# Attention followed by two FFN layers on one Trainium2 core: plain block products in the first set, and its first slot in the attention's tail

## The chip, the cores and the metric

One Trainium2 chip, of which the kernel uses 1 core. The metric is the device time of one execution in microseconds (us). The kernel before takes 961.27 us in the median of 3 runs (960.77 to 962.35).

## The reference

Forgetting attention over 4 batches, 8 heads, 576 tokens and 64 features per head, then two feed-forward layers without biases over the 2304 tokens of width 512, with 2048 hidden features each. All data are float32.

```python
# attention, per batch and head
scores = (q @ k.T) / 8 + cum[:, None] - cum[None, :]    # cum = cumsum(log(clip(f)))
attn = softmax(scores with the upper triangle masked)
x = attn @ v                                            # laid out as 2304 tokens x 512
# first layer
h = x @ w_in                                            # 2304 x 2048
x = (h - tanh(h)) @ w_out
# second layer
h = x @ w_in2
out = (h * sigmoid(h)) @ w_out2
```

## The kernel before

**Precision.** Every operand of a feed-forward product is split into a high part (rounded to the matmul's reduced float32) and a low part, the remainder. Each product is three matmuls: high by high, high by low, low by high. Making the split costs a copy with rounding on ScalarE (`xo` L270, `wh` L188, `gh` L393) and a subtraction on VectorE (`xo` L271, `wl` L190, `gl` L397).

**Attention.** `attention` (L465) walks over 16 pairs of heads, 9 score tiles to a pair, in one loop over steps `n` (L818). Scores on TensorE (L579, L587), row minima on VectorE (L600), exponentials on ScalarE (L608), scaling by the row sums on GpSimd (L622), transposes on TensorE (L634) whose results VectorE and ScalarE copy out (`ptf`, L679), products with the values on TensorE (L690), and a copy into `x` (L698). Steps past the last tile form its tail: the last pairs' transposes and values. The table `ahead` (L790) hangs other work on steps counted from the end of the tiles (`n - N`): loading and decoding the first weights, opening pools in the room that the attention gives up, making the first operands, and the first pieces of the first slot (`next, first`).

**Weights.** They arrive as 64-bit numbers and are decoded by `wjob` (L146): `scale` on ScalarE (L153), `shift`, `exponent`, `low` and `join` on VectorE (L157 to L172), then the splits `hi` and `lo`. For `w_in`, four sums of blocks come between (`sum`, L177). One *pair* of weights (index `q`) is 256 hidden features: `w_in` (m = 0) and `w_out` (m = 1). Two pairs make a *set*; a layer has four sets.

**Slots.** A *unit* is one set by one block of 768 tokens, so a set has three units, and layer 1 and layer 2 have twelve each. A *slot* is one unit by one pair; there are 48 slots, numbered from 0, so the first set is slots 0 to 5. In each slot the product of `w_in` with `x` is cut into 2 by 2 blocks and done in Winograd's form with **seven** block products (`product`, L366; six matmuls of 384 columns each) instead of eight: seven sums of operands made in advance (`xtemp`, `xmake`: `xt` L257, `xo` L270 and L271) and seven additions per slot on VectorE behind the products (`add`, L407) plus one copy on ScalarE (L435). `bend` (L381) applies tanh to a half of 768 elements (L384) and subtracts (L386). Eight steps of the second product (`project`, L322, six matmuls each) of the slot before stand between the block products, as the letters P and G in `slot_steps` (L409) say:

```python
pieces = "P1 G P6 G P2 G G P7 G P5 G P4 G P3 G".split()
if sl == 0:
    pieces = "P1 P2 P6 G G G G P7 G P5 G P4 G P3 G".split()
```

In slot 0 nothing is there to project, in slot 1 only two of the eight steps are. The seven operands of a block are made once, in the first set, spilled to DRAM (`xd`, L273), and reloaded for the later sets (`xload`, L278).

**What sets the order.** The program is scheduled by hand: every engine and every DMA queue runs its instructions in the order in which the code emits them. `fills` hands out the decoding of later weights to positions in slots, `xplan` (filled by `xat`, L287 on) the making and reloading of operands. All bulk transfers stand in the queue of SyncE (SP).

## Time and profile before

| | |
|---|---|
| runs, median of 3 | 961.27 us (960.77 to 962.35) |
| the profiled execution, its own time | 961.22 us |
| its span in the profile | 959.4 us |
| mean granted TensorE clock | 0.995 |
| PE busy | 930.7 us (97%) |
| VectorE (DVE) busy | 741.3 us (77%) |
| ScalarE (ACT) busy | 438.1 us (46%) |
| GpSimd (POOL) busy | 161.2 us (17%) |
| DMA engines, mean busy share of the main queue | 53.7% |
| of the chain that ended last: PE, DVE, ACT | 84%, 9%, 3% |

The profiled execution's own time is 1.8 us more than its span. PE is TensorE's matmuls, PEld its weight loads; a matmul's end is modelled, so matmuls that follow one another overlap in the table, and the spacing of starts tells the rate. The attention takes the first 180 us or so, the first layer runs to about 570 us, and the second layer takes the rest.

### The profile page before, as it was taken

What the parts mean: (1) busy time and instruction counts of PE and PEld (TensorE: products, weight loads), DVE (VectorE), ACT (ScalarE), POOL (GpSimd) and SP (SyncE); (2) the same over time, 40 slices, a digit from 0 to 9 for tenths busy, and PEclk for the clock granted to TensorE, in tenths of its full rate; (3) what the DMA queues carried; (4) which work ended last, traced back from release to release, by engine and by line L of the source; (5) the groups of instructions that cost most, each with busy time, mean ns of one, the idle gap of its engine ahead of it and who ended that gap; (6) DMA issues with size and microseconds to landing.
All of it is one profiled execution on the core that took longest, in us unless ns stands there. A gap on an engine that the chain in (4) does not pass through costs nothing.

```text
span 959.4 us, 14837 instructions
## 1 busy us (share of the span) xinstructions
PE 930.7 (97%) x5496; PEld 844.5 (88%) x5496; DVE 741.3 (77%) x1338; ACT 438.1 (46%) x782; POOL 161.2 (17%) x242
## 2 busy tenths in 40 slices
PE   8999999769999999999999989999999999999998
PEld 6777776559999999999999989898998999898996
DVE  7788887888897887888788988877767677764543
ACT  6788879445554332424233435564423243332311
POOL 8999998200000000000000000000000000000000
PEclk9999999998999999999999999999999999999999
DMA  5344353544576565756585354657756485437622
GB/s 172 135 131 133 112 174 125 208 176 173 235 283 242 180 237 208 275 184 234 174 314 196 136 210 153 230 218 275 306 187 213 164 315 209 161 135 230 236 94 98
DMA packets 45800, 188.86 MB, mean 197 GB/s; under 512 B 9440, under 2 KB 9440, under 8 KB 45696
## 3 DMA queue, kind: packets, MB, share of 16 engines
q1 hardware_dynamic: 45720, 187.90, 53.7%
q8 instruction: 43, 0.70, 0.3%
q14 instruction: 29, 0.24, 0.1%
q10 hardware_dynamic: 8, 0.02, 0.0%
HBM read 148.44 MB, written 38.34 MB: 195 GB/s over the span
## 4 chain that ended last, share of the span: by engine, by line
PE 84%; DVE 9%; ACT 3%; issue 2%; POOL 1%; DMA 1%; ACTq 0%; POOLq 0%; DVEq 0%
PE a L342 37%; PE h L374 32%; PE t L634 4%; PE s L587 4%; PE out_t L690 4%; DVE hs L407 2%; PE s L579 2%; DVE xo L271 1%; ACT t L384 1%; DVE wl L190 1%; DVE xt L257 1%; ACT xo L270 1%; DVE t L386 1%; POOL p L622 1%; ACT wh L188 1%
## 5 line engine op out<-in xcount | busy, mean ns | idle before, releaser
L374 PE MATMUL h<-xo,wh 128*128 128x384 f32 x1344 | 346.2, 338 | 12.1 <-DVE hs L407 6.9
L374 PEld LDWEIGHTS h<-xo,wh 128*128 128x128 f32 x1344 | 246.7, 189 | 29.6 <-DVE hs L407 7.2
L407 DVE TENSOR_TENSOR hs<-h,hs 128x384 f32<-128x384 f32 x336 | 186.0, 554 | 87.1 <-PE h L374 82.0
L384 ACT ACTIVATE t<-hs 128x768 f32<-128x768 f32 x96 | 81.3, 847 | 339.7 <-DVE hs L407 339.4
L374 PE MATMUL h<-xo,wl 128*128 128x384 f32 x672 | 226.6, 337 | 0.0
L342 PE MATMUL a<-gh,wl 128*128 128x384 f32 x384 | 129.2, 337 | 2.6 <-DVE wl L190 2.6
L342 PE MATMUL a<-gl,wh 128*128 128x384 f32 x384 | 129.0, 336 | 1.9 <-DVE gl L397 1.9
L342 PE MATMUL a<-gh,wh 128*128 128x384 f32 x384 | 129.2, 336 | 0.3 <-DVE x L358 0.3
L374 PEld LDWEIGHTS h<-xo,wl 128*128 128x128 f32 x672 | 126.9, 189 | 0.0
L397 DVE TENSOR_TENSOR gl<-t,gh 128x768 fp32r<-128x768 f32 x96 | 91.6, 954 | 37.6 <-ACT gh L393 37.4
L342 PE MATMUL a<-wh,gl 128*128 128x512 f32 x288 | 114.1, 396 | 0.0
L342 PE MATMUL a<-wl,gh 128*128 128x512 f32 x288 | 113.8, 395 | 0.0
L342 PE MATMUL a<-wh,gh 128*128 128x512 f32 x288 | 112.1, 389 | 0.6 <-DVE ob L362 0.6
L393 ACT CAST gh<-t 128x768 fp32r<-128x768 f32 x96 | 80.3, 837 | 29.6 <-DVE t L386 28.5
L608 ACT ACTIVATE p<-p,mn 128x128 f32<-128x128 f32 (+3 forms) x128 | 71.3, 559 | 14.7 <-DVE mn L600 12.6
L342 PEld LDWEIGHTS a<-gh,wl 128*128 128x128 f32 x384 | 72.6, 189 | 2.9 <-DVE wl L190 2.9
L600 DVE CUSTOM_DVE_ANT_0 p<-s,mask 128x128 f32<-128x128 f32 (+3 forms) x128 | 59.5, 480 | 19.9 <-PE s L587 19.9
L342 PEld LDWEIGHTS a<-gl,wh 128*128 128x128 f32 x384 | 72.5, 189 | 2.1 <-DVE gl L397 2.1
L622 POOL TENSOR_SCALAR p<-p,sm 128x128 f32<-128x128 f32 (+3 forms) x128 | 72.1, 581 | 11.6 <-DVE sm L619 11.5
L342 PEld LDWEIGHTS a<-gh,wh 128*128 128x128 f32 x384 | 72.6, 189 | 1.0 <-DVE x L358 0.9
L386 DVE TENSOR_TENSOR t<-hs,t 128x768 f32<-128x768 f32 x48 | 46.0, 958 | 25.5 <-ACT t L384 23.3
L342 PEld LDWEIGHTS a<-wh,gl 128*128 128x128 f32 x288 | 54.0, 187 | 11.6
(90 smaller groups left out, 1230.9 us busy)
## 6 DMA issues: line engine op xcount, KB each, us to landing
xo<-xd SPq DMA_DIRECT2D x126, 768.0 KB
xd<-xo SPq DMA_DIRECT2D x42, 768.0 KB
raw<-w_in SPq DMA_DIRECT2D x32, 512.0 KB
raw<-w_out SPq DMA_DIRECT2D x32, 512.0 KB
kqraw<-kq SPq DMA_DIRECT2D x16, 608.0 KB
vraw<-v SPq DMA_DIRECT2D x16, 320.0 KB
out<-ob SPq DMA_DIRECT2D x6, 512.0 KB
out<-ob SPq DMA_DIRECT2D x6, 256.0 KB
```

The costliest lines, as they stand in the source:

```text
L342: nc.tensor.matmul(dst, w, m, start=first and r == 0, stop=last and r == 2)
L374: nc.tensor.matmul(dst, w[:, ks], m[:, k], start=k == 0 and r == 0, stop=k == 1 and r == 2)
L384: nc.scalar.activation(t, hs[h], AF.Silu if l else AF.Tanh)
L386: nc.vector.tensor_tensor(t, hs[h], t, ALU.subtract)
L393: nc.scalar.copy(gh, hs[h])
L397: nc.vector.tensor_tensor(gl, hs[h], rd(gh), ALU.subtract)
L407: nc.vector.tensor_tensor(to, p, s, ALU.add)
L587: nc.tensor.matmul(s[:, h, c:c + n], a[half(h), q], b[half(h), 0:n], start=r == 0, stop=r == 3,)
L600: nc.vector.tensor_tensor_reduce(out=pt.rearrange("p (g c) -> p g c", g=2) if i == 4 else pt, in0=src, in1=m, op0=ALU.add, op1=ALU.min, sc ...
L608: nc.scalar.activation(pt, pt, AF.Exp, bias=mn, scale=-1.0, accum_out=sums[:, n // 3 % 5, n % 3, 0:1],)
L622: nc.gpsimd.tensor_scalar(pt, pt, sm[:, j:j + 1], 1.0, ALU.mult, ALU.mult)
L634: nc.tensor.transpose(t[:, k], pt[:, c * P:c * P + P], ident)
```

## The change

It does five things, all around the first set.

1. In slots 0 to 5 the 2 by 2 blocks are multiplied plainly: **eight** block products (`plain`), accumulated two by two in PSUM, with no sums of weights, no sums of operands and no additions behind them. tanh and the subtraction now work on quarters of 384 elements straight from PSUM. The order of pieces in these slots is one product, one G, eight times.
2. All of slot 0 is emitted inside the attention's tail (16 pieces instead of 3), and with it three operands that are blocks of `x` (operand 0 is new, held in the tile of operand 7).
3. The decoding of the second pair moves: its `w_in` into the attention's steps (in halves of 512 elements), its `w_out` into the tail. The loads of the first four weights are asked for earlier, and the block sums of the first two pairs are gone.
4. The seven Winograd operands are still made and spilled, for the later sets, but spread over slots 0 to 4 (`STAGED`, `STAGED_AT`), partly in other operands' tiles: operand 5 of the first unit in tile 6, operand 7 always in tile 5.
5. The reloads of the fourth unit (in slot 5) are asked for in the order 6, 4, 1, 5, 2, 7, 3. Pools open at other steps, and some are split.

```diff
         e, o, k = 2 * s + 2, 2 * s + 3, 6 * s
...
+        if s == 0:
+            plan = {
+                1: jobs(e, 0, SCALING, PRE[:2]),
+                2: jobs(e, 0, PRE[2:], SUMS),
+                3: jobs(e, 0, HILO) + jobs(e, 1, SCALING, PRE[:1]),
+                4: jobs(e, 1, PRE[1:], LAST),
+                5: jobs(o, 0, SCALING, PRE, SUMS, HILO) + jobs(o, 1, SCALING),
+                6: jobs(o, 1, PRE),
+            }
...
-    fills[0] = jobs(1, 1, [("scale",)], PRE)
-    fills[1] = jobs(1, 1, LAST)
...
+    STAGED = ((xtemp, 1), (xmake, 5), (xtemp, 2), (xmake, 6), (xtemp, 4), (xmake, 4), (xtemp, 3), (xmake, 7, None, 5))
+    STAGED_AT = (
+        (None, None, None, None, (1, 1), (1, 3), (1, 6), (1, 9)),
+        ((2, 3), (2, 5), (2, 9), (2, 11), (2, 13), (2, 15), (3, 1), (3, 3)),
+        ((3, 10), (3, 12), (4, 1), (4, 3), (4, 5), (4, 7), (4, 9), (4, 11)),
+    )
...
     for u, (l, s, b) in enumerate(units):
-        if u == 0:
+        if u < NB:
+            if u:
+                for p, i, *place in ((5, 1), (7, 2), (13, 0, None, 7), (15, 3)):
+                    xat(2 * u - 1, p, xmake, u, i, *place)
+            for k, to in enumerate(STAGED_AT[u]):
+                if to:
+                    xat(*to, *staged(u, k))
+            continue
+        if u == NB:
+            for i, p in ((6, 0), (4, 1), (1, 4), (5, 5), (2, 6), (7, 12), (3, 14)):
+                xat(2 * u - 1, p, xload, u, i)
             continue
...
+    def plain(u, j, r, h, k):
+        q = 2 * (u // NB) + j
+        c = ((1, 2), (3, 0))[r][k]
+        wih, wil = (w[:, c] for w in wtiles[q, 0])
+        xh, xl = (xo[u, ((1, 7), (2, 3))[k][h]][:, e] for e in range(2))
+        if k == 0:
+            hs[h, r] = pools["ps_h"].tile([P, 512], F32, tag="h", name=f"h{u}_{j}_{h}_{r}")[:, 0:TH]
+        dst = hs[h, r]
+        for d in range(2):
+            ds = slice(d * P, d * P + P)
+            for n, (w, m) in enumerate(((wih, xh), (wih, xl), (wil, xh))):
+                nc.tensor.matmul(dst, w[:, ds], m[:, d], start=k == d == n == 0, stop=k == d == 1 and n == 2)
+        if k == 0:
+            return
+        if r == 0:
+            hs[h] = pools["tp"].tile([P, 2, TH], F32, tag=f"t{h}", name=f"t{u}_{j}_{h}")
+        t = hs[h][:, 1 - r]
+        nc.scalar.activation(t, dst, AF.Tanh)
+        nc.vector.tensor_tensor(t, dst, t, ALU.subtract)
...
-        if sl == 0:
-            pieces = "P1 P2 P6 G G G G P7 G P5 G P4 G P3 G".split()
+        if u < NB:
+            pieces = [c for r in ("000", "001", "100", "101", "010", "011", "110", "111") for c in (r, "G")]
...
+            elif u < NB:
+                r, h, k = map(int, what)
+                plain(u, j, r, h, k)
+                if p == 0:
+                    rest()
+                elif p in (6, 14):
+                    left.extend([(high, (u, j, h)), (low, (u, j, h))])
+                    if p == 6:
+                        rest()
...
-            for n, q, m, i in ((27, 0, 0, 0), (31, 0, 0, 1), (54, 0, 1, 0), (58, 0, 1, 1), (112, 1, 0, 0),
-                               (114, 1, 0, 1), (121, 1, 1, 0), (123, 1, 1, 1)):
+            for n, q, m, i in ((22, 0, 0, 0), (24, 0, 0, 1), (54, 0, 1, 0), (58, 0, 1, 1), (85, 1, 0, 0),
+                               (87, 1, 0, 1), (112, 1, 1, 0), (114, 1, 1, 1)):
...
+            todo = jobs(0, 0, scales, both, PLAIN) + jobs(0, 1, scales, both)
+            todo += [(0, 1, w, i) for w in ("hi", "lo") for i in range(2)] + jobs(1, 0, scales, both)
             for k, job in enumerate(todo):
-                at(NTILE * (4 + k // 3) + (1, 3, 5)[k % 3] - N, wjob, *job)
+                at(NTILE * (3 + k // 3) + (1, 3, 5)[k % 3] - N, wjob, *job)
...
+            inner = {
+                2: jobs(1, 0, PLAIN[:1]), 3: jobs(1, 1, SCALING) + jobs(1, 0, PLAIN[1:2]),
+                4: jobs(1, 0, PLAIN[2:]) + jobs(1, 1, PRE[:1]), 5: jobs(1, 1, PRE[1:2]),
+                6: jobs(1, 1, PRE[2:3]), 7: jobs(1, 1, PRE[3:]),
+            }
...
+            for n, k in ((3, 2), (4, 4), (5, 2), (6, 3), (7, 2), (8, 3)):
+                for _ in range(k):
+                    at(n, next, first)
```

**TensorE in the tail, around the values of the last pair.** Names: `h` is a product's result, `t_3` the last pair's last transposes, `out_15` and `out_t` the last pair's products with the values (`ptf` by `vraw`). Before, three block products stand ahead of them and the fourth (`h_0_7`) follows:

```order
L634 MATMUL t_3_1_2920<-ident,pt_1_107 128x128
L374 MATMUL h_0_6_2935<-xo_6_2865,wh_0_1579 128x384 x2
L374 MATMUL h_0_6_2935<-xo_6_2865,wl_0_1580 128x384
L374 MATMUL h_0_6_2935<-xo_6_2865,wh_0_1579 128x384 x2
L374 MATMUL h_0_6_2935<-xo_6_2865,wl_0_1580 128x384
L690 MATMUL out_15_2943<-ptf_110,vraw_2689 64x64 x2
L690 MATMUL out_t<-ptf_110,vraw_2689 64x512 x2
L690 MATMUL out_t<-ptf_110,vraw_2689 64x448 x2
L690 MATMUL out_t<-ptf_110,vraw_2689 64x320 x2
L690 MATMUL out_t<-ptf_110,vraw_2689 64x192 x2
L690 MATMUL out_t<-ptf_110,vraw_2689 64x64 x2
L374 MATMUL h_0_7_3002<-xo_7_2959,wh_0_1579 128x384 x2
```

With the change (`h_0_1_0` is half 1, row 0 of slot 0; lines have moved):

```order
L423 MATMUL h_0_1_0_2974<-xo_7_2838,wl_0_1200 128x384
L423 MATMUL h_0_1_0_2974<-xo_3_2875,wh_0_1199 128x384 x2
L423 MATMUL h_0_1_0_2974<-xo_3_2875,wl_0_1200 128x384
L423 MATMUL h_0_1_0_2974<-xo_3_2875,wh_0_1199 128x384 x2
L423 MATMUL h_0_1_0_2974<-xo_3_2875,wl_0_1200 128x384
L747 MATMUL out_15_2990<-ptf_105,vraw_2694 64x64 x2
L747 MATMUL out_t<-ptf_105,vraw_2694 64x512 x2
L747 MATMUL out_t<-ptf_105,vraw_2694 64x448 x2
L747 MATMUL out_t<-ptf_105,vraw_2694 64x320 x2
L747 MATMUL out_t<-ptf_105,vraw_2694 64x192 x2
L747 MATMUL out_t<-ptf_105,vraw_2694 64x64 x2
L423 MATMUL h_0_1_1_3004<-xo_7_2838,wh_0_1199 128x384 x2
```

Six of slot 0's eight products stand ahead of the last values, and the other two behind them; before it was three of seven.

**VectorE at the end of slot 1, before.** Names: `hs` and `t` are the halves of h and of its tanh, `gl` the low part of the activation, `xo_*` the operands of the second unit, `wl_1_3100` the low part of the second pair's `w_out`:

```order
L386 TENSOR_TENSOR t_1_0_3133<-hs_1_0_3062,t_1_0_3133 128x768
L271 TENSOR_TENSOR xo_5_3136<-xt_1_1_3082,xo_5_3136 128x768
L257 TENSOR_TENSOR xt_1_1_3082<-x 128x768
L407 TENSOR_TENSOR hs_1_1_3080<-h_1_3_3149,hs_1_1_3080 128x384
L397 TENSOR_TENSOR gl_1_0_3158<-t_1_0_3133,gh_1_0_3157 128x768
L386 TENSOR_TENSOR t_1_1_3161<-hs_1_1_3080,t_1_1_3161 128x768
L271 TENSOR_TENSOR xo_7_3164<-xt_1_1_3082,xo_7_3164 128x768
L190 TENSOR_TENSOR wl_1_3100<-wa_1_3020,wh_1_3099 128x1024
L397 TENSOR_TENSOR gl_1_1_3187<-t_1_1_3161,gh_1_1_3186 128x768
L271 TENSOR_TENSOR xo_4_3190<-xt_1_2_3084,xo_4_3190 128x768
L407 TENSOR_TENSOR hs_0_1_3208<-h_0_6_3201,hs_0_0_3184 128x384
L271 TENSOR_TENSOR xo_3_3210<-x,xo_3_3210 128x768
```

With the change the low part of the second pair's `w_out` (`wl_1_3052`) is in slot 0, before slot 0's second `gl`, and the operands near it (`xt_0_2`, `xo_6`) are the first unit's, for the later sets:

```order
L452 TENSOR_TENSOR gl_0_0_2963<-t_0_0_2928,gh_0_0_2962 128x768
L736 COPY ptf_105<-t_3_1_2943 128x2x64
L164 SCALAR_TENSOR_TENSOR wb_1_2947<-raw_1_2247,wb_1_2947 128x1024
L267 TENSOR_TENSOR xt_0_2_2972<-x,xt_0_1_2897 128x768
L430 TENSOR_TENSOR t_0_1_2987<-h_0_1_0_2974,t_0_1_2987 128x384
L172 TENSOR_TENSOR wa_1_2920<-wa_1_2920,wb_1_2947 128x1024
L281 TENSOR_TENSOR xo_6_3013<-xt_0_2_2972,xo_6_3013 128x768
L430 TENSOR_TENSOR t_0_1_2987<-h_0_1_1_3004,t_0_1_2987 128x384
L193 TENSOR_TENSOR wl_1_3052<-wa_1_2920,wh_1_3051 128x1024
L452 TENSOR_TENSOR gl_0_1_3063<-t_0_1_2987,gh_0_1_3062 128x768
```

The split of that weight has moved from behind slot 1's products, fourth from the end, to the middle of slot 0.

**ScalarE in the tail.** `ptf` are the copies of transposed tiles that the values wait for. Before:

```order
L679 COPY ptf_110<-t_1_0_2870 128x2x2x128
L679 COPY ptf_110<-t_2_0_2894 128x2x2x128
L270 CAST xo_5_2924<-xt_0_1_2834 128x768
L679 COPY ptf_110<-t_3_0_2915 128x4x2x64
L698 COPY x<-out_15_2943 128x64
L698 COPY x<-out_t 128x512
L270 CAST xo_7_2959<-xt_0_1_2834 128x768
L188 CAST wh_0_2986<-ws_0_2882 128x768
L270 CAST xo_4_2989<-xt_0_2_2836 128x768
```

With the change (`t_0_0`, `t_0_1` written from `h` are tanh of slot 0, `gh` its rounding):

```order
L736 COPY ptf_105<-t_1_0_2883 128x2x2x128
L429 ACTIVATE t_0_0_2928<-h_0_0_0_2899 128x384
L736 COPY ptf_105<-t_2_0_2906 128x2x2x128
L280 CAST xo_6_2949<-xt_0_1_2897 128x768
L429 ACTIVATE t_0_0_2928<-h_0_0_1_2931 128x384
L448 CAST gh_0_0_2962<-t_0_0_2928 128x768
L736 COPY ptf_105<-t_3_0_2938 128x4x2x64
L429 ACTIVATE t_0_1_2987<-h_0_1_0_2974 128x384
L755 COPY x<-out_15_2990 128x64
L755 COPY x<-out_t 128x512
L280 CAST xo_6_3013<-xt_0_2_2972 128x768
L429 ACTIVATE t_0_1_2987<-h_0_1_1_3004 128x384
```

Between the copies of `t_1_0` and `t_3_0` there stood one operand's cast; now there are two tanh, a cast and a rounding.

## Rows read from the trace of the kernel before

**Rows 1.** The page: busy time of each engine over the span.

```profile
PE 930.7 (97%) x5496; PEld 844.5 (88%) x5496; DVE 741.3 (77%) x1338; ACT 438.1 (46%) x782; POOL 161.2 (17%) x242
```

**Rows 2.** Busy time by stretch: start:end, length, then busy (instructions) of each engine, clock, DMA.

```profile
138.65:148.54 9.89, 9.89 (x93) 7.46 (x90) 9.55 (x34) 8.37 (x26) 9.81 (x15) 1.00 0.56 170
148.54:158.42 9.88, 9.06 (x84) 6.84 (x80) 7.18 (x27) 9.19 (x26) 9.58 (x13) 1.00 0.30 105
172.30:206.00 33.70, 25.34 (x139) 21.17 (x139) 28.09 (x40) 16.08 (x23) 3.01 (x2) 0.95 0.47 183
206.00:231.00 25.00, 19.18 (x93) 18.38 (x93) 21.16 (x29) 10.73 (x14) 0.00 (x0) 0.86 0.47 190
231.00:246.60 15.60, 15.60 (x92) 15.60 (x91) 14.28 (x22) 10.01 (x14) 0.00 (x0) 1.00 0.58 220
```

**Rows 3.** Waits of PE, 170 to 232 us: total, times, longest.

```profile
PE h L374 <- DVE hs L407: 6.9, 5, 3.4
...
PE a L342 <- DVE wl L190: 2.6, 1, 2.6
...
PE a L342 <- DVE gl L397: 1.9, 1, 1.9
...
PE t L634 <- ACT ptf L679: 0.6, 1, 0.6
```

**Rows 4.** Timeline of PE: start, length, instruction, idle before it.

```profile
165.03 1.25 PE L634 MATMUL t<-ident,p 128*128 128x128 f32 x10
...
172.32 0.85 PE L634 MATMUL t<-ident,p 128*128 128x128 f32 x6 [1.44 <-ACT x L698]
...
178.69 2.76 PE L690 MATMUL out_t<-ptf,vraw 128*64 128x512 f32 x20
...
196.40 1.01 PE L374 MATMUL h<-xo,wh 128*128 128x384 f32 x2 [3.42 <-DVE hs L407]
...
215.10 0.44 PE L342 MATMUL a<-gl,wh 128*128 128x384 f32 x1 [1.88 <-DVE gl L397]
...
218.17 0.69 PE L342 MATMUL a<-gh,wl 128*128 128x384 f32 x1 [2.62 <-DVE wl L190]
```

**Rows 5.** Chain that ended last, third slot's end: start, length, what.

```profile
229.92 1.04 PE a L342 x6
230.96 1.04 PE h L374 x6
```

**Rows 6.** Waits of PE from 231 us to the end.

```profile
PE h L374 <- ACT xo L270: 2.0, 1, 2.0
```

**Rows 7.** Groups by line and shape, whole run: xcount | busy, mean ns | idle.

```profile
L407 DVE TENSOR_TENSOR hs<-h,hs 128x384 f32<-128x384 f32 x336 | 186.0, 554 | 87.1 <-PE h L374 82.0 <-ACT xo L270 1.0
...
L397 DVE TENSOR_TENSOR gl<-t,gh 128x768 fp32r<-128x768 f32 x96 | 91.6, 954 | 37.6 <-ACT gh L393 37.4
...
L384 ACT ACTIVATE t<-hs 128x768 f32<-128x768 f32 x96 | 81.3, 847 | 339.7 <-DVE hs L407 339.4 <-ACT gh L393 0.3
...
L386 DVE TENSOR_TENSOR t<-hs,t 128x768 f32<-128x768 f32 x48 | 46.0, 958 | 25.5 <-ACT t L384 23.3
...
L177 DVE TENSOR_TENSOR ws<-ws 128x256 f32<-128x256 f32 x64 | 26.7, 438 | 0.3
...
L271 DVE TENSOR_TENSOR xo<-xt,xo 128x768 fp32r<-128x768 f32 x24 | 22.9, 956 | 4.8 <-ACT xo L270 4.8
...
L435 ACT COPY hs<-h 128x384 f32<-128x384 f32 x48 | 22.5, 468 | 5.9 <-PE h L374 5.6
...
L164 DVE SCALAR_TENSOR_TENSOR wb<-raw,wb 128x1024 f32<-128x1024 uint32 x30 | 36.9, 1230 | 0.5
...
L190 DVE TENSOR_TENSOR wl<-wa,wh 128x1024 fp32r<-128x1024 f32 x15 | 18.3, 1219 | 1.3 <-ACT wh L188 1.3
...
L164 DVE SCALAR_TENSOR_TENSOR wb<-raw,wb 128x512 f32<-128x512 uint32 x4 | 3.5, 868 | 0.0
```

**Rows 8.** Chain that ended last, a spill to DRAM: start, length, what.

```profile
212.75 3.29 DMA xd<-xo
```

More of the change, by code (lines that the diff above doesn't have):

```diff
@@ L59, in forgetting_attention_two_ffn @@
     dram = ctx.enter_context(tc.tile_pool(name="dram", bufs=1, space=bass.MemoryType.DRAM))
-    wpool = {0: ctx.enter_context(tc.tile_pool(name="wp0", bufs=1))}
+    wpool = dict.fromkeys(((0, 0), (0, 1)), ctx.enter_context(tc.tile_pool(name="wp0", bufs=1)))
     def rd(ap):
@@ L181, in wjob @@
                 wtiles[q, m] = [
-                    wpool[q % NSLOT].tile(shape, F32R, tag=f"w{s}{q % NSLOT}_{m}", name=f"w{s}{n}") for s in "hl"
+                    wpool[q % NSLOT, m].tile(shape, F32R, tag=f"w{s}{q % NSLOT}_{m}", name=f"w{s}{n}") for s in "hl"
                 ]
@@ L185, in wjob @@
             frm = st["s"][:, 1:8] if m == 0 else st["w"]
-            c = i if m else (slice(0, 3), slice(3, 7), slice(3, 5), slice(5, 7))[part]
+            c = i if m else (slice(0, 3), slice(3, 7), slice(3, 4))[part]
+            if m == 0 and part == 2:
+                frm = st["s"][:, 0:1]
+            frm = frm if m == 0 and part == 2 else frm[:, c]
             if what == "hi":
-                nc.scalar.copy(hi[:, c], frm[:, c])
+                nc.scalar.copy(hi[:, c], frm)
             else:
-                nc.vector.tensor_tensor(lo[:, c], frm[:, c], rd(hi[:, c]), ALU.subtract)
+                nc.vector.tensor_tensor(lo[:, c], frm, rd(hi[:, c]), ALU.subtract)
     PRE = [(w,) for w in ("shift", "exponent", "low", "join")]
@@ L390, in high @@
         slot = gfree.pop(0)
-        gh, gl = (pools["gp"].tile([P, 2, TH], F32R, tag=f"g{s}{slot}", name=f"g{s}{u}_{j}_{h}") for s in "hl")
+        gh, gl = (pools[f"gp{slot // 2}"].tile([P, 2, TH], F32R, tag=f"g{s}{slot}", name=f"g{s}{u}_{j}_{h}") for s in "hl")
         gt[u, j, h] = gh, gl, slot
@@ L466, in attention @@
         with ExitStack() as actx:
-            early, earlier = (actx.enter_context(ExitStack()) for _ in range(2))
+            mid, early, earlier = (actx.enter_context(ExitStack()) for _ in range(3))
             def pool(stack, name, bufs=1, **kw):
@@ L486, in attention @@
             raw, vraw, kqs = {}, {}, {}
+            ptfs = [pl.tile([P, 2, NPT], F32, name=f"ptf{i}") for i, pl in ((1, ptps[1]), (0, ptps[0]))][::-1]
             des = [kp.tile([P, S + 512], F32R, name=f"de{i}") for i in range(2)]
@@ L494, in attention @@
             out_0 = {}
-            ptfs = [ptp.tile([P, 2, NPT], F32, name=f"ptf{i}") for i in range(2)]
             def half(h):
@@ L814, in attention @@
-            for job in jobs(1, 0, SUMS):
-                at(6, fill, job)
-            for n in (3, 4, 6):
-                at(n, next, first)
+                at(NTILE * (3 + k // 3) + (1, 3, 5)[k % 3] - N, wjob, *job)
+            for n, i, eng, place in ((-11, 1, nc.gpsimd, 1), (-8, 2, nc.gpsimd, 2), (1, 0, None, 7), (2, 3, None, 3)):
+                at(n, xmake, 0, i, eng, place)
+            at(-2, wload, 2, 0)
+            inner = {
[3 more added lines that the diff above has]
+            }
@@ L847, in forgetting_attention_two_ffn @@
         attention(slots[0])
-        for (q, m, *what), i in zip(jobs(1, 0, HILO), (4, None, 3, None)):
-            wjob(q, m, *what)
-            if i:
-                xmake(0, i)
+        for job in jobs(1, 1, LAST):
+            wjob(*job)
         for slot in slots:
```

86 lines of the change are left out of this document (43 added, 43 removed).

## Prediction

> **What bounds the kernel now.** I read the busy line of the page first: TensorE is busy 97% of the span and no other engine over 77% [rows 1]. So the question is where TensorE is not served, and whether the change serves it there. The busy time by stretch answers the first half [rows 2]. In the attention TensorE is full in a pair's 9.89 us (the pair at 138.65), and from 231 us on it is full again. Between 172.3 and 231.0 it is not: 25.3 of 33.7 us, then 19.2 of 25.0. VectorE is at 28.1 and 21.2 us there, the highest of the others. After 231 us TensorE's longest wait is one of 2.0 us, at the second layer's start [rows 6], which the change does not touch.
>
> The waits of TensorE between 170 and 232 us name VectorE: 6.9 us for the additions behind the products (`hs`), 2.6 us for the split of the second pair's `w_out` (`wl`), 1.9 us for the low part of an activation (`gl`) [rows 3]. The timeline shows the long ones at 196.40, 215.10 and 218.17 us [rows 4]. It also shows the clock: the mean granted clock is 0.95 and 0.86 in the two stretches and 1.00 after them [rows 2]. It fell to its lower level, 1.2 GHz, after TensorE had waited 3.42 us at 196.40, and again after the waits before 218.17.
>
> What TensorE's work in this place needs comes from its own rate. Six matmuls of 384 columns take 1.04 us at the full 2.4 GHz [rows 5], so one takes 0.1733 us. From 172.32 us, where the last pair's second transposes start [rows 4], to 230.96 us, where the third slot's last six matmuls have ended and the fourth slot starts [rows 5], the program has 19 transposes (10 took 1.25 us, so 2.4 us), the last pair's values (0.17 us and 2.76, 2.9 us) [rows 4], and 186 matmuls: 42 + 42 + 42 block products and 12 + 48 projections, 32.2 us. That is 37.5 us of work in 58.6 us. **21.1 us are lost to waiting and to the slow clock.**
>
> **The change, part by part.**
>
> *Eight products for seven.* Six slots get 6 matmuls more each: 36 by 0.1733 = 6.2 us more for TensorE. 18 of them (3.1 us) lie in slots 0 to 2, in the stretch that loses 21.1 us; the other 18 (3.1 us) lie in slots 3 to 5, where TensorE is full, and they cost what they take.
>
> *Additions gone.* Each of the six slots loses seven additions of 554 ns, and two subtractions of 958 ns become four on quarters, which I price by the addition that also reads PSUM, 554 ns [rows 7]: 3.9 + 1.9 - 2.2 = 3.6 us less on VectorE per slot, 21.5 us in all. ScalarE loses a copy of 468 ns and two tanh of 847 ns, and gets four of a quarter. A quarter's tanh is nowhere in the trace: the copy of the same 384 elements from PSUM took 468 ns, half of a whole tanh is 424. I take 468, so 1.9 us replace 2.2.
>
> A rule weighs in here against the change. The rows say that two quarters cost VectorE 1.1 us where the whole cost 0.96. The Trainium skill (Perfetto Trace Analysis, section Optimizing Scalar/DVE Operations) says that each ScalarE and VectorE instruction pays a fixed access cost and that larger operations pay where such an engine is saturated. By that rule alone, cutting the tanh work would lose about 0.3 us of VectorE per slot; by the rows the seven additions that go outweigh it twelve times, and the sum keeps the rows.
>
> *Operands and sums.* Eight block sums of weights of 438 ns go (3.5 us). Three splits of operand 0 come, 956 ns each on VectorE (2.9 us) [rows 7]. The seven Winograd operands per block are still made, but no product of the first set waits for them, so they may be late; their cover is the set itself, and if it is gone the fourth unit's reloads in slot 5 are late.
>
> *The second pair's decoding.* Its `w_in` goes into the attention's last four pairs in halves, at most three instructions a pair; a half's costliest step is 868 ns where a whole one took 1230 [rows 7]. Three such are 2.6 us. I cost them at nothing, because the pair at 138.65 already carries three decoding steps and keeps its 9.89 us, and in the one that follows VectorE is busy only 7.2 of 9.88 us [rows 2]. Without that cover it would be up to 2.6 us for each of two pairs. Its `w_out` goes into the tail: the split that TensorE waited 2.62 us for at 218.17 [rows 4] is emitted a slot and a half earlier and stops being a wait.
>
> *Slot 0 in the tail.* On TensorE 36 instead of 18 matmuls stand ahead of the last values (3.1 us more), so these end later. Only the room that they free waits for them, and the data of the first units are of batches done long before. On ScalarE two tanh and a rounding now stand in front of the copy `t_3_0` that the values need. Going through the queue from 172.3 us with the durations of [rows 7], the copy is done about when TensorE comes to the values, so that wait is a few tenths. The one like it before was 0.6 us [rows 3].
>
> *SP's queue.* It holds 64 weight loads, 42 spills and 126 reloads as before. A weight load that waits for its room has behind it only spills that VectorE makes later still.
>
> **The sum.** VectorE's 35 instructions from 172.7 us to slot 1's end: 8 quarters (4.4), 4 `gl` (3.8), 8 operand splits (7.6), 3 operand sums (2.9), copies of the tail (1.4), weight splits (2.5), decoding (5.2): 27.8 us. TensorE's work there is 2.4 + 2.9 + 108 by 0.1733 = 24.0 us. So VectorE is the longer one by 4 us, but its last ten instructions serve products half a slot or more later, and in slot 2 it has some 14 us against TensorE's 16.6 (96 matmuls). The one place with little room is the second unit's second operand, VectorE's 27th instruction: 21.5 us of work after 172.7 is 194.2 us, and TensorE wants it two products into slot 2, at 172.3 + 24.0 + 2.1 = 198.4. VectorE lost 5.6 us to waits in this stretch before (33.7 - 28.1 [rows 2]); as much again makes 199.8, 1.4 us late. With 0.6 us for the copy in the tail I keep **2.0 us** of waiting.
>
> TensorE then reaches the end of slot 2 at 172.3 + 37.5 + 3.1 + 2.0 = 214.9 us instead of 230.96. What followed took 959.4 - 230.96 = 728.4 us, and gets 3.1 us more: 946.5 us of span. With the 1.8 us that lie around it this execution would have taken **948.3 us** instead of 961.22; the median of the runs shown, 961.27, is the same within 0.05. With no wait at all it is 946.3. If the wait of 1.44 us at 172.32 for ScalarE [rows 4], where a different cast now stands in the way, went too, 944.9: the low end.
>
> **The rivals.**
>
> *A wait takes the old one's place.* ScalarE and VectorE alternate within each quarter (tanh, subtraction, rounding, low part), each in order, so one late operand holds up the next quarter. For it: VectorE is still the longer engine in slots 0 and 1. If TensorE waits as at 215.10 and 218.17 (1.9 + 2.6 us), and its clock falls as there, it also pays 2.7 us for the clock (the third slot's 25.0 us less 15.6 of work, less 1.5, 2.2 and 2.9 us of gaps). That is 7.2 us: 946.3 + 7.2 = 953.5. Against it: four PSUM buffers let TensorE run half a slot ahead.
>
> *Late reloads.* The first operand that slot 6 needs is now third in line instead of first, behind operands 6 and 4 and two weight loads. A transfer of this size took 3.29 us on the chain [rows 8]. One such late: 948.3 + 3.3 = 951.6. Against it: 11 us of slot 5 are left after its request.
>
> *Slower.* A staging tile is written again while its spill is under way: tile 6 once in slot 0, tile 5 four times in slots 1 to 4. The cast that rewrites it waits in ScalarE's queue with the tanh behind it. If each of the five waited a whole transfer and TensorE with it, that is 5 by 3.29 = 16.5 us: 948.3 + 16.5 = 964.8. It decides from 3 us a piece on, where it eats the gain. For it: the chain itself runs over such a spill [rows 8]. Against it: eight VectorE instructions, some 6 us, lie between the two writes of tile 6, and more between the others.
>
> *It only moves the loss.* TensorE gets its 6.2 us and VectorE's relief turns into waits for ScalarE of the size of the gain: 961.
>
> **How the numbers follow.** The forecast (945 to 950) has 0.68, because its gain is TensorE's own lost time, counted from two points of the timeline. The wait in the old one's place has 0.17, late reloads 0.07, slower 0.04, no difference 0.04. 0.2% (1.9 us) is about what a measurement of this kernel can tell from no change. Faster is 0.68 + 0.17 + 0.07 = 0.92, the same 0.04, slower 0.04. The range goes from 944.9, the sum without either wait, to 954.5, just over the first rival; it leaves out the last two cases and the edges.
>
> **What would show it.** Right: the stretch from 172 to 231 us has TensorE full from the first slot's end, with no granted clock under 1.00; no wait for `hs` or for the second pair's `wl`; TensorE's matmul count up by 36; the pairs of the attention still 9.89 us. Wrong: waits of TensorE over 2 us in slots 1 and 2, for `xo` or for PSUM freed by the quarter subtractions; a wait for a reload at slot 6's start; casts of operands 5 and 6 on ScalarE that wait for a DMA; a longer pair in the attention's last four.

## The result, and the profile after

The changed kernel took **948.51 us** (median of 4 runs, 948.34 to 949.93) where the kernel before, on the same chip, took 961.81 us (4 runs, 960.77 to 964.13): a ratio of 0.9864, 95% interval 0.9851 to 0.9877, 13.3 us less. Forecast were 948.3 us, faster. The profiled execution took 948.34 us with a span of 946.3 us.

The page's busy line and the busy time by stretch, in the columns of [rows 1] and [rows 2]. The first two stretches are the two pairs of the attention; the next three are what lies between the last pair's second transposes and slot 1, then slot 1, then slot 2.

```profile
PE 932.3 (99%) x5532; PEld 848.5 (90%) x5532; DVE 720.1 (76%) x1306; ACT 437.8 (46%) x791; POOL 159.4 (17%) x242
```

```profile
138.65:148.54 9.89, 9.89 (x93) 7.46 (x91) 8.84 (x33) 8.06 (x26) 9.21 (x15) 1.00 0.39 126
148.54:158.42 9.88, 9.06 (x83) 6.85 (x80) 8.82 (x30) 8.52 (x24) 9.88 (x13) 1.00 0.10 37
171.22:185.35 14.13, 13.95 (x91) 11.88 (x92) 12.00 (x17) 8.34 (x17) 2.01 (x2) 1.00 0.41 162
185.35:195.75 10.40, 10.40 (x61) 10.40 (x61) 7.32 (x10) 7.14 (x10) 0.00 (x0) 1.00 0.57 230
195.75:213.49 17.74, 16.93 (x98) 16.61 (x98) 16.40 (x24) 9.46 (x15) 0.00 (x0) 1.00 0.65 256
```

TensorE has 36 instructions more, VectorE 32 fewer. The pairs keep their 9.89 us. Slots 0 to 2, where the clock had been granted at 0.95 and 0.86 [rows 2], now run at 1.00, and slot 1 is full. TensorE's waits in this place, to be read against [rows 3]:

```profile
PE a L377 <- ACT x L391: 0.8, 1, 0.8
PE t L691 <- DVE ptf L736: 0.6, 1, 0.6
PE out_t L747 <- ACT ptf L736: 0.2, 1, 0.2
```

The waits for `hs`, `wl` and `gl` are gone, and so is one that [rows 3] does not show, of 1.57 us at 183.01 for ScalarE's cast of an operand:

```profile
183.01 0.44 PE L374 MATMUL h<-xo,wh 128*128 128x384 f32 x1 [1.57 <-ACT xo L270]
```

The timeline of TensorE places the three that are left, and two more at the second layer's start, which answer to [rows 6]:

```profile
171.22 1.04 PE L691 MATMUL t<-ident,p 128*128 128x128 f32 x6 [0.64 <-DVE ptf L736]
...
180.43 2.81 PE L747 MATMUL out_t<-ptf,vraw 128*64 128x512 f32 x20 [0.18 <-ACT ptf L736]
...
210.25 0.44 PE L377 MATMUL a<-gh,wh 128*128 128x384 f32 x1 [0.81 <-ACT x L391]
...
554.26 0.45 PE L409 MATMUL h<-xo,wh 128*128 128x384 f32 x1 [2.03 <-ACT xo L280]
555.25 0.69 PE L409 MATMUL h<-xo,wh 128*128 128x384 f32 x1 [0.55 <-DVE xo L281]
```

The tanh and the subtraction of a quarter, in the columns of [rows 7]:

```profile
L430 DVE TENSOR_TENSOR t<-h,t 128x384 f32<-128x384 f32 x24 | 13.3, 554 | 3.8 <-ACT t L429 3.7
L429 ACT ACTIVATE t<-h 128x384 f32<-128x384 f32 x24 | 11.8, 490 | 9.6 <-PE h L423 9.4
```

**Where the time went.** The last pair's second transposes start at 171.22 us, 1.1 us sooner than in [rows 4]. The chain that ended last puts the end of slot 2 at 213.65 us, where it stood at 230.96 [rows 5] (the timeline has both 0.16 us sooner, at 213.49 and 230.80):

```profile
213.65 1.04 PE h L423 x6
```

From 171.22 on that is 42.4 us for 40.7 us of work (the 37.5 us of before and 18 matmuls). So 1.8 us are lost where 21.1 were. After that the 18 matmuls of slots 3 to 5 cost 3.1 us. The same product that waits at the second layer's start came at 568.71 us before and comes at 554.26 now: 14.45 us sooner. From there to the end it is 390.7 us before and 392.0 now: 1.35 us are given back behind that wait, and 13.1 us of span are left.

The time from that product to the end is used below as a second measure: "layer change" is when it starts, in the one profiled execution of each kernel. It leaves out what happens behind it, which varies (last section). The medians include it: a run without the fall of the clock behind the layer change is shorter by a us or more, and the changed kernel's four runs all have a mean granted clock of 0.998 or less.

### The profile page after: what moved, and what is told of

The parts are those of the page before. It is cut to its first block, busy times and chain, and to the rows that moved or that the text cites. A ratio compares the mean times of both kernels' runs of the same rounds, so it can differ in the third digit from the quotient of the medians.

```text
span 946.3 us, 14874 instructions
## 1 busy us (share of the span) xinstructions
PE 932.3 (99%) x5532; PEld 848.5 (90%) x5532; DVE 720.1 (76%) x1306; ACT 437.8 (46%) x791; POOL 159.4 (17%) x242
## 4 chain that ended last, share of the span: by engine, by line
PE 85%; DVE 7%; POOL 3%; ACT 2%; issue 2%; DMA 1%; SPq 0%; DVEq 0%; ACTq 0%; POOLq 0%
PE a L377 38%; PE h L409 30%; PE t L691 4%; PE s L644 4%; PE out_t L747 4%; PE h L423 3%; PE s L636 2%; DVE xo L281 1%; POOL p L679 1%; DVE hs L462 1%; POOL kqs L586 1%; DMA xo<-xd 1%; DVE xt L267 1%; DVE gl L452 1%; ACT xo L280 1%
## 5 line engine op out<-in xcount | busy, mean ns | idle before, releaser
L409 PE MATMUL h<-xo,wh 128*128 128x384 f32 x1176 | 300.9, 336 | 3.1 <-ACT xo L280 2.0
L409 PEld LDWEIGHTS h<-xo,wh 128*128 128x128 f32 x1176 | 215.7, 188 | 18.2 <-ACT xo L280 2.6
L462 DVE TENSOR_TENSOR hs<-h,hs 128x384 f32<-128x384 f32 x294 | 163.0, 555 | 88.9 <-PE h L409 85.2
L439 ACT ACTIVATE t<-hs 128x768 f32<-128x768 f32 x84 | 71.2, 847 | 312.5 <-DVE hs L462 312.5
L409 PE MATMUL h<-xo,wl 128*128 128x384 f32 x588 | 197.9, 336 | 0.0
L409 PEld LDWEIGHTS h<-xo,wl 128*128 128x128 f32 x588 | 110.7, 188 | 0.0
L448 ACT CAST gh<-t 128x768 fp32r<-128x768 f32 x96 | 80.3, 837 | 35.7 <-DVE t L441 23.8
L665 ACT ACTIVATE p<-p,mn 128x128 f32<-128x128 f32 (+3 forms) x128 | 71.2, 558 | 15.6 <-DVE mn L657 12.6
L393 DVE TENSOR_TENSOR x<-a,x 128x768 f32<-128x768 f32 (+2 forms) x60 | 57.1, 951 | 9.4 <-PE a L377 9.3
```

What stands on the lines that cost most here:

```text
L393: nc.vector.tensor_tensor(total, acc, total, ALU.add)
L409: nc.tensor.matmul(dst, w[:, ks], m[:, k], start=k == 0 and r == 0, stop=k == 1 and r == 2)
L439: nc.scalar.activation(t, hs[h], AF.Silu if l else AF.Tanh)
L448: nc.scalar.copy(gh, hs[h])
L462: nc.vector.tensor_tensor(to, p, s, ALU.add)
L665: nc.scalar.activation(pt, pt, AF.Exp, bias=mn, scale=-1.0, accum_out=sums[:, n // 3 % 5, n % 3, 0:1],)
```

## The experiments

| kernel | median, us | before on the same chip, us | layer change, us | from there to the end, us |
|---|---|---|---|---|
| before | 961.81 | | 568.71 | 390.7 |
| changed | 948.51 | 961.81 | 554.26 | 392.0 |
| e1, before without the second `w_out` decoding | 957.69 | 962.05 | 563.72 | 392.3 |
| e2, and without the second `w_in` decoding | 953.28 | 962.05 | 560.92 | 390.7 |
| e3, changed with 8 additions a slot | 953.85 | 962.05 | 560.84 | 390.7 |
| e4, changed with 4 additions a slot | 949.33 | 962.05 | 557.89 | 390.7 |
| e5, changed, `w_out` decoded late | 948.90 | 961.45 | 554.63 | 393.6 |
| e6, changed, three products in the tail | 948.37 | 961.45 | 555.62 | 392.2 |
| e7, changed, 18 more matmuls | 951.73 | 961.45 | 557.37 | 392.2 |
| e8, changed, reloads in the old order | 948.75 | 961.45 | 555.59 | 392.3 |
| e9, as e3, staging moved later | 954.71 | 961.80 | 560.61 | 392.2 |
| e10, changed, `w_in` decoded in the tail | 949.59 | 961.80 | 555.14 | 392.3 |
| e11, plain products without the moves | 952.59 | 961.63 | 558.33 | 392.3 |
| v12, staging and second layer's operands moved | 945.80 | 961.80 | no such wait | |

**Does the decoding's work, taken away, bring the gain without plain products?** In the kernel before, for e1 (e2 lists both tiles and drops the two splits behind the attention too):

```
     def fill(j):
         q, m, *what = j
+        if (q, m) in ((1, 1),):
+            if what[0] == "low":
+                raws.pop((q, m))
+                wload(q + 1, m)
+            return
...
-        woh, wol = (w[:, i] for w in wtiles[2 * (u // NB) + j, 1])
+        woh, wol = (w[:, i] for w in wtiles[2 * (u // NB) + j * (u >= NB), 1])
```

> The kernel before, with the decoding of the second pair's w_out left out (its two weight tiles are those of the first pair, so the output is not the reference's; the weight loads and every product stay). VectorE loses two steps of 0.69 us and three of 1.22 us, 5.0 us, all in slots 0 and 1. Theory (in slots 0 to 2 TensorE waits for VectorE, whoever its work belongs to): the 2.62 us wait for wl goes, and with 5.0 us less in front of the additions TensorE gains 4 to 8 us (up to 2.7 us of that from the clock): 953 to 957. Rival (the chain of additions behind the products holds TensorE, not the sum of VectorE's work): only the 2.62 us go, 958.5 or more, and the waits for hs stay at 6.9 us.

> As the run before, and the decoding and block sums of the second pair's w_in left out too (its products use the first pair's operands; the output is not the reference's). VectorE loses another 0.69 x 2 + 1.23 x 2 + four sums of 0.44 + two splits of 0.87 and 1.15, 7.6 us, so 12.6 us in all between 161 and 230 us. Theory (VectorE's work counts, the decoding's as much as the additions'): gain of 12 to 20 us, 941 to 949, with the clock at 1.00 in the third slot. Rival A (the additions are the cause, the decoding only lies beside them): 954 or more, with waits for hs of over 4 us left. Rival B (the decoding's move alone made the whole gain of the change, the plain products none): 949 or less here as well; it parts from the theory in the next two runs.

e1 took 957.69 us (0.9954 of before, 0.9939 to 0.9969) and e2 953.28 us (0.9908, 0.9892 to 0.9925). TensorE's waits from 170 to 232 us in e1, then in e2:

```profile
PE h L379 <- DVE hs L412: 4.2, 4, 2.6
PE a L347 <- DVE gl L402: 1.9, 1, 1.9
```

```profile
PE h L379 <- DVE hs L412: 2.4, 1, 2.4
PE a L347 <- DVE gl L402: 1.4, 1, 1.4
```

In e1 `wl` is gone and `hs` fell from 6.9 us [rows 3] to 4.2; the layer change comes 5.0 us sooner. So VectorE's work counts whoever it belongs to, and the rival of e1 falls. The time is 0.7 us outside the range that I gave. In e2, 12.6 us less work gave 7.8 us at the layer change and 8.8 in time: less than the theory, a little more than rival A, and far from rival B. Even without any decoding of the second pair, the additions still hold TensorE for 2.4 us in one piece.

That e1's 5.0 us less work gave 5.0 us is the net of two larger changes, as the start of slot 3 in the timeline says; before, e1 and e2:

```profile
230.80 0.51 PE L374 MATMUL h<-xo,wh 128*128 128x384 f32 x2
```

```profile
221.51 0.51 PE L379 MATMUL h<-xo,wh 128*128 128x384 f32 x2
```

```profile
218.35 0.51 PE L379 MATMUL h<-xo,wh 128*128 128x384 f32 x2
```

Up to there e1 gains 9.3 us (its clock is granted at 1.00 all through slots 0 to 2) and e2 12.5. Then e1 loses 4.3 us again, and e2 4.7, most of it (3.5 and 3.7 us) to waits that the kernel before does not have. The larger two of e2, from its waits between 165 and 300 us:

```profile
PE a L347 <- ACT x L361: 3.1, 2, 1.6
```

They stand at 232.49 and 298.02 us, for ScalarE's copy of the projections' sums, and `gl` waits of 0.36 and 0.24 us come on top; e1 has the same four (1.24, 1.64, 0.37 and 0.22 us). Ahead of e2's first, ScalarE's rounding of a weight waits 2.36 us for VectorE, so VectorE's lag seems to stand behind it again. Ahead of the second, such a rounding waits 7.49 us for TensorE's projections, where the kernel before waits 0.4 at most. The edit of e1 and e2 lets the projections read the first pair's tiles for longer; that this causes the second wait is likely and was not tested.

**Is it VectorE's relief?** The changed kernel, with the relief given back (e3 does it twice per quarter, e4 once):

```
         nc.vector.tensor_tensor(t, dst, t, ALU.subtract)
+        if 2 * u + j < 3:
...
+            for _ in range(2):
+                nc.vector.tensor_tensor(zs[0], zs[0], zs[0], ALU.add)
```

> The changed kernel with VectorE's relief given back: in slots 0 to 2 two additions of 128x384 on a scratch tile of their own follow each quarter's subtraction, 8 in a slot at some 0.48 us (estimated as half of a 0.95 us subtraction of 768), 3.8 us a slot, 11.5 us in all; nothing waits for them but VectorE's own queue. VectorE is idle 6.5 of 42.3 us between 171.2 and 213.5 us. Theory: the idle time takes part of it, the rest is TensorE's: 5 to 11 us slower than the changed kernel, 953 to 959, with waits for VectorE's tiles in slots 1 and 2 and perhaps a lower clock. Rival B (the plain products' relief does not matter): under 2 us, 950 or less.

> As the run before with half of it: one such addition behind each quarter's subtraction, 5.8 us in all in slots 0 to 2. Theory: idle time of 6.5 us would take all of it if it lay in the right places; it does not quite, so 0.5 to 3 us slower than the changed kernel: 949 to 951.5. If the margin were none, 5.8 us slower (954). Rival B: no difference, 948.5.

One such addition took 554 ns, not 480, so e3 gives back 13.3 us and e4 6.6. e3 is 5.3 us slower than the changed kernel (6.6 at the layer change), e4 0.8 us (3.6 at the layer change). Rival B falls with e3. e4's own runs were 948.38 and 948.49 us with a mean granted clock of 1.000, and 950.17 and 950.39 with 0.998; its profiled one is the slowest of them, and its clock fell in slot 2. TensorE's longest wait in e3:

```profile
215.47 0.69 PE L377 MATMUL a<-gh,wh 128*128 128x384 f32 x1 [4.07 <-ACT x L391]
```

It is the changed kernel's wait of 0.81 us at 210.25, grown. VectorE was busy 45.62 of 47.48 us there, and the clock fell too:

```profile
171.22:218.70 47.48, 41.60 (x240) 38.90 (x241) 45.62 (x70) 24.53 (x41) 2.38 (x3) 0.96 0.49 194
```

The margin is a few us in three slots, as slots 0 to 2 of the changed kernel say (35.7 of 42.3 us).

e3 gives back more than the 10.8 us (3.6 a slot) at which the prediction priced the relief by the missing additions in slots 0 to 2, and 6.6 of the layer change's 14.45 us go, less than half. So the amount of VectorE's work is a cause, and not the whole. If the parts add up, the moves are some 4 us of the rest (e11, below), and the remaining 3 to 4 us no run isolates. The additions of e3 have nothing waiting for them but VectorE's queue, while TensorE waited for those of the kernel before (`hs`); that this makes the difference is not shown.

**By which road does VectorE's lag reach TensorE?** ScalarE in the changed kernel:

```profile
205.90 0.84 ACT L280 CAST xo<-xt 128x768 fp32r<-128x768 f32 x1 [3.62 <-DVE xt L267]
206.64 0.49 ACT L429 ACTIVATE t<-h 128x384 f32<-128x384 f32 x1
208.66 0.83 ACT L448 CAST gh<-t 128x768 fp32r<-128x768 f32 x1 [1.54 <-DVE t L430]
209.40 0.79 ACT L391 COPY x<-a 128x768 f32<-128x768 f32 x1
```

The copy that frees the accumulator (L391) stands behind a rounding that waits for VectorE's subtraction, and that behind a staging cast that waits for VectorE's `xt`. I took the staging cast for the culprit and moved it in e3's kernel:

```
-        ((2, 3), (2, 5), (2, 9), (2, 11), (2, 13), (2, 15), (3, 1), (3, 3)),
-        ((3, 10), (3, 12), (4, 1), (4, 3), (4, 5), (4, 7), (4, 9), (4, 11)),
+        ((2, 11), (2, 13), (2, 15), (3, 1), (3, 3), (3, 5), (3, 7), (3, 9)),
+        ((3, 12), (3, 14), (4, 1), (4, 3), (4, 5), (4, 7), (4, 9), (4, 11)),
```

> The changed kernel with the same 8 additions a slot on VectorE as in the run with 11.5 us given back, and with the second unit's eight staging steps moved from slots 2 and 3 (first at piece 3 of slot 2) to piece 11 of slot 2 and after, the third unit's first two by two pieces. In the run without the move TensorE's one long wait was 4.07 us at 215.47, for ScalarE's copy of the projections' sums to x (it frees the accumulator), and the changed kernel itself waits 0.81 us there. Theory (VectorE's lag reaches TensorE through ScalarE's order: the copy stands behind staging casts that wait for VectorE): with the staging behind the copy this wait falls under 1.5 us and the run gains 2.5 to 5 us on the one without the move, 949 to 951.5. Rival (VectorE's work alone decides, wherever it stands): the wait changes its name but not its size, within 1.5 us of the run without the move, 952.4 to 955.

```profile
212.38 0.83 ACT L456 CAST gh<-t 128x768 fp32r<-128x768 f32 x1 [6.64 <-DVE t L432]
213.11 0.79 ACT L391 COPY x<-a 128x768 f32<-128x768 f32 x1
```

```profile
213.96 0.44 PE L377 MATMUL a<-gh,wh 128*128 128x384 f32 x1 [2.58 <-ACT x L391]
```

The theory fell. ScalarE no longer waits for `xt`, but now 6.64 us for the subtraction itself. TensorE's wait kept its name and shrank from 4.07 to 2.58 us, others came later (0.53 us at 249.62), and the layer change came 0.23 us sooner than in e3. The run took 954.71 us, within 1 us of e3. The rival was right in time, though not in the size of the wait: where VectorE is full, its work decides.

**The parts of the change, undone one at a time and together.** e5: `w_out` of the second pair decoded in slots 0 and 1, the third pair's `w_in` from slot 2 on. e6: fewer pieces of slot 0 in the tail. e10: the second pair's `w_in` decoded in the tail.

```
-                1: jobs(e, 0, SCALING, PRE[:2]),
-                2: jobs(e, 0, PRE[2:], SUMS),
+                2: jobs(e, 0, SCALING, PRE),
...
+    for (sl, p), job in zip(((0, 7), (0, 9), (0, 10), (0, 11), (0, 12), (1, 5), (1, 14)), jobs(1, 1, SCALING, PRE, LAST)):
+        xat(sl, p, wjob, *job)
```

```
-            for n, k in ((3, 2), (4, 4), (5, 2), (6, 3), (7, 2), (8, 3)):
+            for n, k in ((3, 1), (4, 2), (6, 2)):
```

```
-            todo += [(0, 1, w, i) for w in ("hi", "lo") for i in range(2)] + jobs(1, 0, scales, both)
+            todo += [(0, 1, w, i) for w in ("hi", "lo") for i in range(2)]
...
+            for n, job in zip((-3, -2, -1, 0, 1), jobs(1, 0, SCALING, PRE)):
+                at(n, wjob, *job)
```

> The changed kernel with the decoding of the second pair's w_out put back to slots 0 and 1 (its split at pieces 5 and 14 of slot 1), and that of the third pair's w_in from slots 1 to 3 back to slots 2 to 3, as both stood before the change. The sum of VectorE's work over slots 0 to 2 stays within 1 us. Theory (that sum decides, and the split still comes half a slot before its product): no difference above 1 us, 948 to 949.5. Rival (the early split is a part of the gain by itself): the 2.62 us wait for wl comes back, with the clock's part up to 5 us: 951 to 953.5.

> The changed kernel with only three block products (18 matmuls, as before the change) of slot 0 inside the attention's tail, the other five after it. Theory: TensorE does the same work in another order; the last transposes and values come up to 3.1 us earlier, and wait for their copies about as long as they did before the change (0.6 us instead of 0.2): 0 to 1 us slower, 948.5 to 949.5. Rival (the tail placement gives ScalarE and VectorE a head start that slots 1 and 2 live on): the quarter tanh and subtractions come 3 us later, and TensorE waits 2 us or more in slots 0 to 2: 950.5 or more.

> The changed kernel with the decoding of the second pair's w_in taken out of the attention's last four pairs and put back into its tail (five whole steps from three tiles before the end to one after it), some 3.9 us of VectorE and 1.1 us of ScalarE between 161 and 175 us. Theory: VectorE is busy 6.3 of 9.9 us in 161 to 171 us and takes most of it there; what is left delays the copies that the last transposes wait for: 0 to 2 us slower, 948.5 to 950.5. Rival (this move is a main part of the gain): VectorE enters slot 0 some 4 us later and stays so: 3 to 5 us slower, 951.5 to 953.5.

By their medians e5 and e6 are no different from the changed kernel (948.90 and 948.37 us), and e10 is 1.1 us slower. But the layer change comes 0.4, 1.4 and 0.9 us later in them, and runs with the same mean granted clock agree with that: at 0.998 the changed kernel took 948.34 to 948.52 us, e5 948.68, e6 949.85 and e10 949.57 to 949.92. Three of e6's four runs had the clock at 1.000 (948.08 to 948.38 us), which none of the changed kernel's had. So e5's theory held, e10's held, and e6 costs 1.4 us, over its theory's 0 to 1 and under its rival. In e10 the place is plain:

```profile
172.30 0.85 PE L691 MATMUL t<-ident,p 128*128 128x128 f32 x6 [1.76 <-issue]
```

That is the time of [rows 4] again. So the 1.1 us that the changed kernel gains ahead of slot 0 come from the `w_in` decoding that left the tail.

e11 undoes all three: the edits above together, and it also puts the second pair's `w_in` splits behind the attention, which no other run does. The staging, the reloads' order and the weights without block sums stay as in the changed kernel.

> The plain products alone: the changed kernel with all three moves undone together (the second pair's w_in decoded in the tail and its splits behind the attention, its w_out in slots 0 and 1, the third pair's decoding from slot 2 on, three block products of slot 0 in the tail). Undone one at a time, the layer change came 0.9, 0.4 and 1.4 us later than in the changed kernel. Theory (the plain products and the operands that they need no sums for make most of the gain; the moves are worth little each and add up): 2.6 us slower than the changed kernel, 950 to 952.5. Rival (any one of the moves gives VectorE the head start, and the others stood in for the one undone): without all three the waits for VectorE in slots 1 and 2 come back with the clock's fall, 954 or more.

952.59 us, 0.1 us over the theory's range and 1.4 under the rival's. The plain products without the moves gain 9.0 us of the 13.3, the moves together 4.1. At the layer change the moves together are worth 4.1 us as well, and undone one at a time 0.4, 1.4 and 0.9, 2.6 in all. Whether the other 1.5 us come from moves that stand in for one another, or from the `w_in` splits, is open. TensorE's longest waits from 170 to 232 us in e11, where the clock is granted at 1.00 throughout:

```profile
PE h L426 <- DVE xo L280: 2.1, 2, 1.6
PE t L694 <- POOL p L682: 1.2, 1, 1.2
PE t L694 <- ACT ptf L739: 0.6, 1, 0.6
PE a L380 <- DVE wl L193: 0.3, 1, 0.3
```

**What do the added matmuls cost where TensorE is full?** The first six of slots 3, 4 and 5 done twice:

```
         dst = hs[h, r]
+        if (r, h, k) == (0, 0, 0) and 2 * u + j > 2:
+            for d in range(2):
+                for n, (w, m) in enumerate(((wih, xh), (wih, xl), (wil, xh))):
+                    nc.tensor.matmul(dst, w[:, d * P:d * P + P], m[:, d], start=d == n == 0, stop=d == 1 and n == 2)
```

> The changed kernel with six more matmuls in each of slots 3 to 5 (the first six of the slot are done twice, the second time from a cleared accumulator), 18 in all, at 0.1733 us. Theory of the sum (TensorE is full there, so the eighth product costs what it takes): 3.1 us slower, 951.6. Rival (slack in slots 3 to 5 takes them): under 1 us, 949.5 or less.

3.2 us slower in time, 3.11 us at the layer change: 0.173 us each, what they take. Nothing hides them.

**The reloads' order.**

```
-            for i, p in ((6, 0), (4, 1), (1, 4), (5, 5), (2, 6), (7, 12), (3, 14)):
+            for i, p in ((1, 4), (6, 5), (2, 6), (5, 9), (4, 11), (7, 12), (3, 14)):
```

> The changed kernel with the fourth unit's reloads asked for in the old order as far as the tiles allow (1, 6, 2, 5, 4, 7, 3, with the first request at piece 4 of slot 5 instead of piece 0). Theory: the order costs and gives nothing, slot 6 starts without a wait either way: 948.5, within 0.6 us. Rival: the queue of 16 transfers is close to late, and a request that comes four pieces later makes TensorE wait in slot 6 by up to 3.3 us: 949.5 to 951.8.

By the medians nothing can be told apart (948.75 us). The trace shows one wait, in slot 6, which the changed kernel does not have:

```profile
271.92 0.59 PE L409 MATMUL h<-xo,wh 128*128 128x384 f32 x2 [1.05 <-DMA xo<-xd]
```

It ends 8.5 us into slot 6 (which starts at 263.42 us in this view), after seven pieces of 1.04 us, so the product that waits is the one with operand 7. That operand is asked for at piece 12 in both; here two requests that the change puts at pieces 1 and 5 stand just ahead of it. The layer change comes 1.33 us later. The two runs with a mean granted clock of 0.998 took 949.61 and 949.94 us, 1.1 us or more above the changed kernel's at that clock; the other two, at 1.000, took 947.88 and 947.90 and bring the median down. So the reordering guards some 1.3 us, and the rival was right: a request that comes later makes TensorE wait in slot 6.

**A version that beats both.** e9's staging move, and the second layer's first operands 5 and 7 a slot sooner:

```
+            if b == 0:
+                xat(2 * u - 1, 11, xmake, u, 5)
+                xat(2 * u - 1, 12, xtemp, l, b, 3)
+                xat(2 * u - 1, 13, xmake, u, 7)
```

> A version to beat both: the changed kernel with the second unit's staging moved as above, and at the second layer's start the first unit's operand 5, the sum behind it and operand 7 made in the slot before (pieces 11 to 13, as the first layer's other sets do) instead of at the start of their own slot. Theory: the wait of 0.81 us at 210.25 goes; TensorE's waits of 2.03 and 0.55 us at 554 us go, and with them the fall of the clock that followed them in some profiles (the span behind that point was 390.7 us in four of them and 392.0 or more in six): 3.4 to 4.9 us faster than the changed kernel, 943.6 to 945.1. Rival: VectorE is nearly full in that slot too, and what is done earlier there delays the additions by as much; the waits come back as waits for hs: 946.5 to 949.

**945.80 us** (945.66 to 945.93, 4 runs), 0.9828 of before (0.9810 to 0.9846), 2.7 us under the changed kernel's median. The wait at 210 us is gone, those of 2.03 and 0.55 us are gone, and three others came around the second layer's start:

```profile
540.96 0.44 PE L383 MATMUL a<-gh,wh 128*128 128x384 f32 x1 [0.32 <-DVE x L399]
...
558.22 0.45 PE L383 MATMUL a<-gh,wh 128*128 128x384 f32 x1 [1.33 <-DVE x L399]
...
574.53 0.50 PE L383 MATMUL a<-wh,gh 128*128 128x512 f32 x1 [0.43 <-DVE x L399]
```

So 2.1 of the 2.6 us of waiting there came back under another name, as the rival said, though not for `hs`; the time lies between the two. Slot 3 starts 1.0 us sooner than in the changed kernel, and of the 1.6 us of span won behind it 0.5 are waiting; about 1.1 us are left for the clock, which is granted at 1.00 there (an estimate from these differences).

## Why the prediction was right, step by step

- **TensorE's 21.1 lost us are what the change can win.** Right: 1.8 us are left, and its clock there is 1.00. With the 1.1 us ahead of slot 0 that is 20.4 us won; 6.2 us of matmuls off it are 14.2, and the layer change moved by 14.45 (a wait of 0.26 us at 555.98 before is gone too).
- **36 matmuls cost 6.2 us, 3.1 of them in full.** Right; e7 measured such 18 at 3.11 us.
- **VectorE's relief.** Right as a cause, but not the only one. The quarter subtraction took 554 ns, as priced; the quarter tanh 490, where I took 468. The rule on fixed costs per instruction that I weighed against the change (the Trainium skill, Perfetto Trace Analysis, section Optimizing Scalar/DVE Operations) shows in these rows with the size that I gave it, 0.3 us a slot: four quarter subtractions are 2.2 us, two of halves were 1.9. e1 to e4 show that work taken from VectorE or given to it in slots 0 to 2 moves the time, and not one to one: by the start of slot 3, 5.0 us taken gave 9.3 (the clock no longer fell) and 12.6 gave 12.5, of which 4.3 and 4.7 were lost again behind it; 13.3 us given cost 6.6.
- **Which part brings it.** I let additions, sums and moves work together and did not say how the gain divides. e11 does: 9.0 us plain products with what belongs to them, 4.1 the moves.
- **The decoding in the attention is free.** Right for the pairs (9.89 us still). But I missed what its leaving the tail gives: my sum kept the 1.44 us wait at 172.32, and only the low end of the range let it go. It fell to 0.64 us at 171.22, and e10 brought the old time back.
- **The 2.0 us of residual waiting.** The size was nearly right (1.8), the place wrong, so the size is luck. I had the second unit's operand 2 arrive at 199.8 us, by charging 5.6 us of VectorE's idle time. Its split ended at 197.74, 0.09 us before TensorE came for it (195.75 + 2.08 = 197.83, one product and one projection into slot 2). The wait came at 210.25 us, for ScalarE's copy of the sums, a piece of ScalarE's queue that my working did not go through in slot 2. I gave VectorE some 14 us in that slot; it was busy 16.40 of its 17.74 us, so the room that I saw there was not there.
- **What follows slot 2.** I took 728.4 us and 3.1 more; it was 732.7, 1.1 more: 1.35 from the clock's fall at the layer change, less the 0.26 us wait. Slot 2 ended 1.3 us sooner than I said (213.65 for 214.9). **That the sum met the profiled time to 0.1 us, and the median to 0.2, is two misses that cancel.**
- **Rivals.** A wait in the old one's place: it is there, 0.81 us, with no fall of the clock; e3 shows it at full size (4.07 us, then the clock at its lower level). Late reloads: none; e8 shows where one would come, at operand 7 and not at the first. The staging tile's spill: no cast of ScalarE waited for a transfer in slots 0 to 5. No difference: out.

What stays open: what makes up the 3 to 4 us of the gain that neither the amount of VectorE's work (e3) nor the moves (e11) account for. The order in which VectorE's work stands ahead of what TensorE waits for is the candidate that was not run by itself.

## What to carry to other kernels

Where an engine that is not the longest over the whole run is full in one stretch, work taken from it there is worth it even at the price of work on the longest engine, as long as that added work falls into time that was lost anyway; where TensorE is full, each added matmul costs what it takes. Several small moves that by their medians seem worth little when undone alone were worth 4 us together, so undo them together, and compare runs of the same granted clock, before calling them idle. An engine's waits that go in one stretch can come back in the next: e1 and e2 lost 4.3 and 4.7 us of the 9.3 and 12.5 that they had won. A sum that agrees to 0.1 us is to be compared stage by stage before it is believed.
